# Strided scaling into token order, whole-tile stores, and a 384/128 split of the last rows, in a sliding-window attention + SwiGLU kernel

## The chip, the cores and the metric

The kernel runs on one core of a Trainium2 chip. The metric is device time in microseconds (us) of one execution; smaller is better. The five engines are named as in the profile: PE (matrix multiply), PEld (its weight loads), DVE (vector engine), ACT (scalar engine), POOL (GpSimd), SP (the engine that only issues transfers here). A "q" after a name (SPq, ACTq) is that engine's instruction queue.

## What is computed

```python
# q, k, v: (8 batches, 8 heads, 576 positions, 64), fp32
scores = q @ k.T / sqrt(64), kept where 0 <= i - j < 64, else -1e9
attn   = softmax(scores) @ v                      # (8, 8, 576, 64)
x      = attn with heads joined                   # (4608 tokens, 512)
g      = x @ w_gate ; val = x @ w_val             # (4608, 1536)
out    = (g * sigmoid(g) * val) @ w_out           # (4608, 512), fp32
```

## The kernel before

The 4608 tokens are nine tiles of 512. Tile 0 to 6 take the first 512 positions of batches 0 to 6, tile 7 (`LAST`) takes the last 64 positions of all eight batches, and tile 8 takes the first 512 positions of batch 7. Each tile passes through three stages:

1. **Attention.** `scores` (line 244) makes the exponentials of the scores, `sums` (309) or `sums_wide` (318) the reciprocal row sums `r`, and `mix_all` (371) multiplies the exponentials by the values. Its result `ao_ps` lies in PSUM as fp32, one 128x512 piece for each of four pairs of heads `u` (two 64-wide heads on the 128 partitions, 512 tokens along the columns). `scale` (356) then multiplies each piece by `r`, on DVE, into the bf16 tile `xT[t][:, u, :]`. One line does it, 359.
2. **Gate and value.** `gate_value` (397) runs for `m` = 0 to 11: four matmuls of 512 columns with `wg` and four with `wv` (line 401), one for each `c` = `u` of `xT`; ACT applies silu (394), and DVE multiplies into `hT` (395). The first four matmuls of a tile therefore need the four scaled pieces in the order in which they are made.
3. **Projection.** `project` (434) runs for four groups `s` of 128 of the tile's columns: twelve 512-column matmuls with `hT` as weights (410), a copy out of PSUM into `os_` (417), and stores to DRAM (429).

The order is written out by hand (`manual_schedule`). For t = 2 to 8 the loop (lines 652 on) interleaves tile t's attention with tile t-1's projection: `scores(t, 0)`, `project(t-1, 0)`, part of `s = 1`, `scores(t, 1)`, `sums`, the rest of `s = 1`, `project(t-1, 2)`, `sums`, `mix_all(t)`, `project(t-1, 3)`, and then the twelve `gate_value(t, m)`. So the four scales of a tile run on DVE while PE runs the twelve matmuls of `project(t-1, 3)`. For t = 1 the interleaving is written out (lines 638 to 650): behind `mix_all(1)` there are eight projection matmuls (`columns(10, 12)`), then four copies of tile 0's results, two on ACT and two on DVE, and then the gates. Tile 0 is the start of the pipeline, before the loop.

**Order of tokens.** The columns of a tile are not in token order. Tile 0 keeps e-major order with 4 tokens to a group (column = e * 128 + r for token 4r + e). All later tiles (`t >= TURNED`) use 16 (column = e * 32 + r for token 16r + e), which comes from the way the queries are loaded and turned. That order goes on through `ao_ps`, `r`, `xT`, `hT` and the result. A group of 128 columns thus holds four sets of 32 tokens whose rows in DRAM lie 16 apart, and `project_end` (415) writes each group with four stores of 32 rows. All are issued by SP, except that tile 8 alternates SP and ACT.

**The end.** The last 128 columns of tile 8 go through `project_last` (439): two halves of 256 output columns, twelve matmuls each (446), a copy each (450), and four stores of 32 rows each, alternating SP and ACT (453).

PSUM has two buffers each for the tags `g` and `v` (gates, projection) and two double ones for `a` (scores, mixing). `os_` and `r` have four buffers each.

Two operations elsewhere matter for reading the profile: `split_k` (188) copies bf16 from PSUM on DVE with a step of 128 elements in its source, and `turn_k` (207) and `turn_q` (194) transpose 32x32 blocks on DVE, the first with a step of 4 elements in its destination, the second contiguous there. Lines 496 and 612 read the small bf16 tile `tri` in SBUF with a step of 4 and of 16 elements.

Of the kernel before, what the change touches and what calls it, by code (L numbers as in the profile page):

```python
# [8 lines left out]
P = 128  # L9
# [8 lines left out]
def kernel(  # L18
# [10 lines left out]
    nc = tc.nc  # L29
    S, D, H = 576, 64, 8  # L30
    NTOK, DFF, DM = 4608, 1536, 512
    NT = NTOK // 512
    TURNED = 1
    LAST = NT - 2

    ctx.enter_context(tc.manual_schedule())
    cst = ctx.enter_context(tc.tile_pool(name="cst", bufs=1))
# [11 lines left out]
    wo = cst.tile([P, 12, DM], BF16, name="wo")  # L49
# [12 lines left out]
    def batch(t):  # L62
        return t if t < LAST else t - 1

# [6 lines left out]
    staged, queries, weights, inverse, xT, hT = {}, {}, {}, {}, {}, {}  # L71
# [9 lines left out]
    def load_q(t):  # L81
# [3 lines left out]
        for a, c in quarters:  # L85
            p0 = 64 * a + 32 * c
            if t != LAST:
                nc.gpsimd.dma_start(  # L88
# [26 lines left out]
    def load_qk(t):  # L115
        q_s = load_q(t)
        if t == 1:
            staged[t] = q_s, None
            return
        if t == LAST:  # L120
            groups = [(b, S - P) for b in range(4)]
# [122 lines left out]
    def scores(t, w):  # L244
# [3 lines left out]
        for j in range(8):  # L248
            if t == LAST:
                k_j = kT[t % 2 if j < 4 else 2]  # L250
# [4 lines left out]
            for lo, hi, c, src, k0 in pieces:  # L255
                for h in range(2):
                    for x in range(2):
# [11 lines left out]
                        )  # L269
        n = 1024 if t == LAST else 960  # L270
        for h in range(2):
# [8 lines left out]
            both = epool.tile([P, 8, 64], BF16, name="both", tag="both")  # L280
            lo = 2 if t == LAST else 0
            nc.vector.tensor_add(both[:], E[:, 1:17:2], E[:, lo:lo + 15:2])  # L282
# [17 lines left out]
    def room(n):  # L300
        return fsb.tile([P, 2, 512], FP32, name="r", tag="r", bufs=4)[:, 0:n]
# [54 lines left out]
    def scale(t, u, o_ps):  # L356
        if u == 0:
            xT[t] = att.tile([P, 4, 512], BF16, name="xT", tag="xT")
        nc.vector.tensor_mul(xT[t][:, u, :], o_ps, inverse.pop((t, u)))  # L359

    def values_first(u, o_ps):
        mix_first(u, o_ps)
        scale(0, u, o_ps)

    def wide(name):
        return ps_a.tile([P, 2, 512], FP32, name=name, tag="a")
# [4 lines left out]
    def mix_all(t):  # L371
        tiles = wide("ao_ps"), wide("ao_ps")
        for w in range(2):
            mix(t, w, (tiles[w][:, 0], tiles[w][:, 1]))
        for u in range(4):
            scale(t, u, tiles[u // 2][:, u % 2])
# [38 lines left out]
    def project_end(t, s, o_ps, copy=nc.vector.tensor_copy):  # L415
        os_ = fsb.tile([P, 512], FP32, name="os_", tag="os_", bufs=4)
        copy(os_[:], o_ps[:])
        rows = out[S * batch(t):S * batch(t) + 512]
        if t < TURNED:
            nc.sync.dma_start(rows.rearrange("(r e) f -> e r f", e=4)[s], os_[:])  # L420
            return
        if t == LAST:
            rows = out.rearrange("(b s) f -> b s f", s=S)[:, 512:S]
            rows = rows.rearrange("b (r e) f -> e b r f", e=16)
        else:
            rows = rows.rearrange("(r e) f -> e r f", e=16)
        for i in range(4):
            eng = nc.scalar if t == NT - 1 and i % 2 else nc.sync
            eng.dma_start(rows[4 * s + i], os_[32 * i:32 * i + 32])

    def out_tile():
        return ps_f.tile([P, 512], FP32, name="o_ps", tag="g")

    def project(t, s):
        o_ps = out_tile()
        project_part(t, (s,), (o_ps,), range(12))
        project_end(t, s, o_ps)

    def project_last(t, s):
        rows = out[S * batch(t):S * batch(t) + 512].rearrange("(r e) f -> e r f", e=16)  # L440
        os_ = fsb.tile([P, 512], FP32, name="os_", tag="os_", bufs=4)
        tiles = out_tile(), out_tile()
        for x in range(2):
            f = slice(256 * x, 256 * x + 256)
            for c in range(12):
                nc.tensor.matmul(  # L446
                    tiles[x][:, 0:256], hT[t][:, c, P * s:P * s + P], wo[:, c, f],
                    start=(c == 0), stop=(c == 11),
                )
            nc.vector.tensor_copy(os_[:, f], tiles[x][:, 0:256])  # L450
            for i in range(4):
                eng = nc.scalar if i % 2 else nc.sync
                eng.dma_start(rows[4 * s + i][:, f], os_[32 * i:32 * i + 32, f])

    def set_exp():
        nc.scalar.preload_act_table_set("natural_log_exp_and_others")  # L456
# [27 lines left out]
    for a in range(2):  # L484
        tr = tri[64 * a:64 * a + 64]
        nc.gpsimd.affine_select(
            out=tr[:, 1 - a], in_=tr[:, 1 - a], compare_op=ALU.is_ge, fill=0.0,
# [3 lines left out]
            out=tr[:, a], in_=tr[:, a], compare_op=ALU.is_ge, fill=0.0,  # L491
# [78 lines left out]
    d_ps, r = wide("d_ps"), room(2)  # L570
# [33 lines left out]
    for m in range(12):  # L604
# [15 lines left out]
        if 5 <= m < 9:  # L620
            u = m - 5
            join(on_a, keys[:, u], raw_k[:, 2 * u:2 * u + 2])
        if 6 <= m < 10:
            u = m - 6
# [8 lines left out]
    tiles = [ps_f.tile([P, 512], FP32, name="o_ps", tag=x) for x in "gvgv"]  # L633
# [15 lines left out]
    for s in range(4):  # L649
        project_end(0, s, tiles[s], on_a if s < 2 else on_v)  # L650

    for t in range(1, NT):
        if t > 1:
            set_exp()
            scores(t, 0)
            project(t - 1, 0)
            if t == 2:
                stage_v(3)
            o_ps = out_tile()
            project_part(t - 1, (1,), (o_ps,), range(5))  # L660
            scores(t, 1)
            sums(t, 0)
            project_part(t - 1, (1,), (o_ps,), range(5, 12))
            project_end(t - 1, 1, o_ps)
            project(t - 1, 2)
            sums(t, 1)
            mix_all(t)
            project(t - 1, 3)
# [21 lines left out]
    for s in range(3):  # L690
        project(NT - 1, s)
    project_last(NT - 1, 3)

# [28 lines left out]
```

## Time and profile before

| | us |
|---|---|
| median of three runs | 328.64 (328.26 to 329.04) |
| profiled execution, its own time: span from first to last instruction | 326.2 |
| median less span (what lies around the span) | 2.4 |
| PE busy | 315.9 (97%), 2700 matmuls |
| DVE busy | 220.2 (67%) |
| ACT busy | 167.2 (51%) |
| POOL busy | 142.8 (44%) |

The three timed runs list only their times; the profiled execution has no listed time beside its span, so the 2.4 us is taken as constant. The granted TensorE clock is 0.999 of full speed over the span. The chain of work that ended last runs 86% through PE; DMA has 8%, POOL 3% and DVE 1%. PE's busy time counts pipelined matmuls whose ends are modelled, so gaps are best read from starts: in the gates and projections one 512-column matmul follows another every 0.216 us (four take 0.86 us in the chain).

### The profile page before, as it was taken

To read this page: it belongs to the slowest core of one execution; us is meant where nothing else is said; L and a number is where in the kernel's file an instruction comes from. 1 tells how busy PE (TensorE), PEld (TensorE's weight loads), DVE (VectorE), ACT (ScalarE), POOL (GpSimd) and SP (SyncE) were. 2 spreads that over 40 slices of the span, in tenths; PEclk is the share of its full clock that TensorE was granted. 3 is DMA by queue.
4 is the path that set the end of the run, shared out by engine and by line. 5 is a ranking of instruction groups with operands and counts; after the bars stand their busy time and mean duration, and the time that the engine had idled before them with its cause. 6 is when DMAs were issued, how large, how long until landed. Compare 5 with 4: busy or idle time off the path is not lost.

```text
span 326.2 us, 6959 instructions
## 1 busy us (share of the span) xinstructions
PE 315.9 (97%) x2700; PEld 150.7 (46%) x2743; DVE 220.2 (67%) x352; ACT 167.2 (51%) x239; POOL 142.8 (44%) x256
## 2 busy tenths in 40 slices
PE   8899999999999999999999999999999999999995
PEld 3444444444444444444444544454444544444443
DVE  5865755587766776887678766876697586773431
ACT  5855557337733683358336743565347633773300
POOL 5944545986085893586024989464200000000000
PEclk9999999999999999999999999999999999999999
DMA  7999999999789999959812999799401300020013
GB/s 253 200 202 202 206 146 215 170 146 143 164 160 206 138 151 205 192 81 214 175 38 29 169 173 92 53 191 195 97 2 34 99 0 2 16 83 32 2 33 98
DMA packets 82865, 40.84 MB, mean 125 GB/s; under 512 B 64272, under 2 KB 78352, under 8 KB 82832
## 3 DMA queue, kind: packets, MB, share of 16 engines
q0 software_dynamic: 50672, 23.08, 57.7%
q1 hardware_dynamic: 31136, 16.26, 19.3%
q10 hardware_dynamic: 1024, 1.05, 1.1%
q8 instruction: 21, 0.34, 0.4%
q14 instruction: 12, 0.10, 0.1%
HBM read 54.00 MB, written 9.44 MB: 194 GB/s over the span
## 4 chain that ended last, share of the span: by engine, by line
PE 86%; DMA 8%; POOL 3%; issue 1%; DVE 1%; SPq 0%; DVEq 0%; POOLq 0%
PE o_ps L410 28%; PE g_ps L401 26%; PE v_ps L401 25%; DMA wv<-in_moe_w_val_dram 4%; DMA q_s<-in_q_dram 3%; PE s_ps L261 3%; PE ao_ps L347 2%; PE d_ps L294 1%; DMA q_f<-in_q_dram 1%; POOL wg L172 1%; POOL wv L172 1%; PE o_ps L446 1%; POOL v L129 1%; POOL qk_b L517 0%; DVE qT L198 0%
## 5 line engine op out<-in xcount | busy, mean ns | idle before, releaser
L394 ACT ACTIVATE sg<-g_ps 128x512 f32<-128x512 f32 x108 | 64.4, 597 | 113.8 <-PE g_ps L401 85.1
L395 DVE TENSOR_TENSOR hT<-sg,v_ps 128x512 bf16<-128x512 f32 x108 | 74.7, 693 | 59.8 <-PE v_ps L401 49.2
L401 PE MATMUL g_ps<-xT,wg 128*128 128x512 bf16 x415 | 108.2, 379 | 0.9
L401 PE MATMUL v_ps<-xT,wv 128*128 128x512 bf16 x415 | 107.2, 379 | 0.1
L410 PE MATMUL o_ps<-wo,hT 128*128 128x512 bf16 x396 | 93.6, 380 | 1.5 <-issue 0.3
L108 POOL DMA_DIRECT2D k_s<-in_k_dram x112 | 60.6, 552 | 26.2 <-DMA q_s<-in_q_dram 15.3
L401 PEld LDWEIGHTS <-wv 128*128 128x128 bf16 x424 | 41.5, 98 | 50.1
L401 PEld LDWEIGHTS <-wg 128*128 128x128 bf16 x424 | 41.3, 98 | 49.5 <-issue 0.6
L410 PEld LDWEIGHTS <-hT 128*128 128x128 bf16 x420 | 39.1, 98 | 46.5 <-issue 1.8
L274 ACT ACTIVATE eb<-s_ps 128x960 bf16<-128x960 f32 (+1 forms) x32 | 29.5, 974 | 16.4 <-PE s_ps L261 16.3
L208 DVE STREAM_TRANSPOSE kT<-k_s 128x512 bf16<-128x512 bf16 x28 | 36.0, 1284 | 0.3 <-issue 0.3
L277 DVE TENSOR_TENSOR eb<-eb,mask 128x960 bf16<-128x960 bf16 (+1 forms) x32 | 21.1, 658 | 14.4 <-ACT eb L274 14.4
L359 DVE TENSOR_TENSOR xT<-ao_ps,r 128x512 bf16<-128x512 f32 x36 | 23.0, 684 | 6.5 <-PE ao_ps L347 4.8
L162 POOL CAST vb<-v_f 128x512 bf16<-128x512 f32 x20 | 11.4, 618 | 31.9 <-DMA v_f<-in_v_dram 22.1
L304 ACT ACTIVATE r<-d_ps 128x512 f32<-128x512 f32 (+1 forms) x33 | 20.8, 629 | 6.2 <-PE d_ps L294 5.9
L198 DVE STREAM_TRANSPOSE qT<-q_s 128x512 bf16<-128x512 bf16 x32 | 22.4, 702 | 0.8 <-DMA q_s<-in_q_dram 0.8
L307 ACT ACTIVATE r<-r 128x512 f32<-128x512 f32 (+1 forms) x33 | 22.0, 669 | 1.0
L88 POOL DMA_DIRECT2D q_s<-in_q_dram x28 | 15.2, 564 | 10.2 <-DVE qT L198 4.8
L137 POOL DMA_DIRECT2D vb<-in_v_dram x16 | 10.9, 710 | 8.7 <-DMA wo<-in_moe_w_out_dram 3.7
L282 DVE TENSOR_TENSOR both<-eb 128x512 bf16<-128x512 bf16 x32 | 13.6, 425 | 1.1
L456 ACT ACT_TABLE_LOAD x9 | 11.5, 1283 | 2.0 <-issue 1.9
L95 POOL DMA_DIRECT2D q_s<-in_q_dram x16 | 8.6, 629 | 7.4 <-DVE qT L198 7.4
(107 smaller groups left out, 185.2 us busy)
## 6 DMA issues: line engine op xcount, KB each, us to landing
q_s<-in_q_dram POOLq DMA_DIRECT2D x28, 248.0 KB, 6.0
k_s<-in_k_dram POOLq DMA_DIRECT2D x112, 56.0 KB, 4.8
v_f<-in_v_dram SPq DMA_DIRECT2D x40, 128.0 KB
wo<-in_moe_w_out_dram POOLq DMA_DIRECT2D x3, 512.0 KB, 12.3
q_f<-in_q_dram SPq DMA_DIRECT2D x4, 256.0 KB
vb<-in_v_dram POOLq DMA_DIRECT2D x16, 64.0 KB, 2.9
v<-in_v_dram POOLq DMA_DIRECT2D x16, 64.0 KB, 3.1
q_s<-in_q_dram POOLq DMA_DIRECT2D x16, 62.0 KB, 3.6
```

The lines of the kernel that those rows point to most:

```text
L108: nc.gpsimd.dma_start(k_s[p0:p0 + 32, g, :, 0:w], k[b, a:H:2, s:s + P].rearrange("u (r e) d -> r u (e d)", e=4) [:, :, 32 * c:32 * c + w],)
L198: nc.vector.transpose(queries[t][:, u, :].rearrange("r (e x) -> r e x", e=16), staged[t][0][:, u].rearrange("r (e d) -> r e d", d=D)[:, :, ...
L208: nc.vector.transpose(dst[:, u, :].rearrange("r (g x e) -> r g e x", g=4, e=4), k_s[:, :, u].rearrange("r g (e d) -> r g e d", d=D)[:, :, ...
L274: nc.scalar.activation(flat, s_ps[h][:].rearrange("r a b -> r (a b)")[:, 0:n], AF.Exp, scale=0.125)
L277: nc.vector.tensor_mul(flat, flat, mask[:].rearrange("r j c e y -> r (j c e y)")[:, 0:n])
L304: nc.scalar.activation(r, d_ps, AF.Ln)
L307: nc.scalar.activation(r, r, AF.Exp, scale=-1.0)
L359: nc.vector.tensor_mul(xT[t][:, u, :], o_ps, inverse.pop((t, u)))
L394: nc.scalar.activation(sg[:], g_ps[:], AF.Silu)
L395: nc.vector.tensor_mul(hT[t][:, m, :], sg[:], v_ps[:])
L401: nc.tensor.matmul(ps[:], w[:, c, P * m:P * m + P], xT[t][:, c, :], start=(c == 0), stop=(c == 3),)
L410: nc.tensor.matmul(o_ps[:], hT[t][:, c, P * s:P * s + P], wo[:, c, :], start=(c == 0), stop=(c == 11),)
```

## The change

There are three parts. (1) For t >= 1 `scale` reads both of its sources with a step of 32 fp32 elements (128 bytes) and writes `xT` in token order, contiguous. (2) Since the columns then are tokens in order, each group of 128 columns is 128 consecutive rows of the output (in tile 7, two runs of 64), and one store takes them (two in tile 7, and two halves in the cases of `HALVED`), all from SP. (3) The last group's output columns are taken as 384 and 128 instead of 256 and 256, with one store each from SP.

```diff
+    HALVED = [(1, 0), (1, 1), (1, 2), (1, 3), (2, 0)]
...
     def scale(t, u, o_ps):
         if u == 0:
             xT[t] = att.tile([P, 4, 512], BF16, name="xT", tag="xT")
-        nc.vector.tensor_mul(xT[t][:, u, :], o_ps, inverse.pop((t, u)))
+        x, r = xT[t][:, u, :], inverse.pop((t, u))
+        if t < TURNED:
+            nc.vector.tensor_mul(x, o_ps, r)
+            return
+        nc.vector.tensor_mul(
+            x.rearrange("r (x e) -> r x e", e=16),
+            o_ps.rearrange("r (e x) -> r x e", e=16),
+            r.rearrange("r (e x) -> r x e", e=16),
+        )
...
         if t < TURNED:
             nc.sync.dma_start(rows.rearrange("(r e) f -> e r f", e=4)[s], os_[:])
-            return
-        if t == LAST:
-            rows = out.rearrange("(b s) f -> b s f", s=S)[:, 512:S]
-            rows = rows.rearrange("b (r e) f -> e b r f", e=16)
+        elif t == LAST:
+            for i in range(2):
+                r0 = S * (2 * s + i) + 512
+                nc.sync.dma_start(out[r0:r0 + 64], os_[64 * i:64 * i + 64])
         else:
-            rows = rows.rearrange("(r e) f -> e r f", e=16)
-        for i in range(4):
-            eng = nc.scalar if t == NT - 1 and i % 2 else nc.sync
-            eng.dma_start(rows[4 * s + i], os_[32 * i:32 * i + 32])
+            n = 2 if (t, s) in HALVED else 1
+            for i in range(n):
+                r = slice(P // n * i, P // n * (i + 1))
+                nc.sync.dma_start(rows[P * s:P * s + P][r], os_[r])
...
     def project_last(t, s):
-        rows = out[S * batch(t):S * batch(t) + 512].rearrange("(r e) f -> e r f", e=16)
+        r0 = S * batch(t) + P * s
         os_ = fsb.tile([P, 512], FP32, name="os_", tag="os_", bufs=4)
-        tiles = out_tile(), out_tile()
-        for x in range(2):
-            f = slice(256 * x, 256 * x + 256)
+        for f0, f1 in ((0, 384), (384, 512)):
+            o_ps = out_tile()
             for c in range(12):
                 nc.tensor.matmul(
-                    tiles[x][:, 0:256], hT[t][:, c, P * s:P * s + P], wo[:, c, f],
+                    o_ps[:, 0:f1 - f0], hT[t][:, c, P * s:P * s + P], wo[:, c, f0:f1],
                     start=(c == 0), stop=(c == 11),
                 )
-            nc.vector.tensor_copy(os_[:, f], tiles[x][:, 0:256])
-            for i in range(4):
-                eng = nc.scalar if i % 2 else nc.sync
-                eng.dma_start(rows[4 * s + i][:, f], os_[32 * i:32 * i + 32, f])
+            nc.vector.tensor_copy(os_[:, f0:f1], o_ps[:, 0:f1 - f0])
+            nc.sync.dma_start(out[r0:r0 + P, f0:f1], os_[:, f0:f1])
```

## The prediction

> **What bounds the kernel now.** I read the page first: its busy shares and the chain.
>
> ```profile
> PE 315.9 (97%) x2700; PEld 150.7 (46%) x2743; DVE 220.2 (67%) x352; ACT 167.2 (51%) x239; POOL 142.8 (44%) x256
> ...
> PE 86%; DMA 8%; POOL 3%; issue 1%; DVE 1%; SPq 0%; DVEq 0%; POOLq 0%
> ```
>
> PE sets the end; a change gains only where it shortens PE's work, its waits or the tail, and loses wherever it makes PE wait. So I asked next for the waits of PE.
>
> ```profile
> PE s_ps L230 <- DVE kT L189: 1.1, 2, 1.0
> PE g_ps L381 <- DVE xT L359: 0.6, 1, 0.6
> PE o_ps L410 <- issue: 0.3, 2, 0.2
> ```
>
> The columns are total us, times, longest. From tile 1 on PE waits for no scale (the 0.6 is tile 0) and for no store. Merging stores has no PE wait to remove, and the scales are hidden. The timeline shows how well; first tile 2, then tile 1:
>
> ```profile
> 84.30 2.68 DVE L359 TENSOR_TENSOR xT<-ao_ps,r 128x512 bf16<-128x512 f32 x4 [0.16 <-PE ao_ps L347]
> 84.53 2.77 PE L410 MATMUL o_ps<-wo,hT 128*128 128x512 bf16 x11
> 85.62 0.63 ACT L307 ACTIVATE r<-r 128x512 f32<-128x512 f32 x1
> 87.13 1.03 PE L401 MATMUL g_ps<-xT,wg 128*128 128x512 bf16 x4
> 87.33 0.69 DVE L417 COPY os__1355<-o_ps 128x512 f32<-128x512 f32 x1 [0.35 <-PE o_ps L410]
> 89.12 0.69 DVE L395 TENSOR_TENSOR hT<-sg,v_ps 128x512 bf16<-128x512 f32 x1 [1.10 <-PE v_ps L401]
> ```
>
> ```profile
> 51.08 2.48 DVE L359 TENSOR_TENSOR xT<-ao_ps,r 128x512 bf16<-128x512 f32 x4 [3.82 <-PE ao_ps L347]
> 53.24 1.02 PE L401 MATMUL g_ps<-xT,wg 128*128 128x512 bf16 x4
> ```
>
> The columns are start, length, instruction. In tile 2 four scales run from 84.30 to 86.98 under the last projection. The gate starts at 87.13 and needs the fourth scaled piece only at its fourth matmul, three steps of 0.216 later, at 87.78. That leaves 0.80. The 2.68 includes a wait of the fourth scale for ACT's last reciprocal (85.62 + 0.63 = 86.25); back to back four take 2.48, as tile 1 shows, so a scale occupies (2.48 - 0.68) / 3 = 0.60. Tiles 3 to 6 and 8 repeat tile 2 to 0.01 us (tile 8: scales at 288.19, gate at 291.02); tile 7 has scales at 254.17 and gate at 257.12. Tile 1 has least: need at 53.24 + 0.65 = 53.89 against 51.08 + 2.48 = 53.56.
>
> **Part 1, the scale.** Let d be the added time of one scale. With 0.05 to release PE (the last matmul's end and the last copy's start lie that close in the tail), the fourth scale releases at S + 2.48 + 4d + 0.05, S being the first scale's start; PE wants it at G + 0.65, G being the gate's. The stall is 4d - 0.95 in tiles 2 to 6 and 8 (G - S = 2.83), 4d - 1.07 in tile 7 (2.95), 4d - 0.28 in tile 1 (2.16), never below zero. Up to d = 0.24 only tile 1 pays.
>
> No row shows an fp32 read in SBUF with a large step. The nearest, by length (L359 itself: 668/680/692):
>
> ```profile
> L208 DVE STREAM_TRANSPOSE kT<-k_s 128x512 bf16<-128x512 bf16 x28 | 36.0, 1284 | 0.3 <-issue 0.3
> L198 DVE STREAM_TRANSPOSE qT<-q_s 128x512 bf16<-128x512 bf16 x32 | 22.4, 702 | 0.8 <-DMA q_s<-in_q_dram 0.8
> L189 DVE COPY kT<-tp 128x512 bf16<-128x512 bf16 x8 | 5.5, 682 | 0.6 <-PE tp L186 0.6
> L450 DVE COPY os__4457<-o_ps 128x256 f32<-128x256 f32 x2 | 0.8, 424 | 1.5 <-PE o_ps L446 1.5
> ```
>
> ```profile
> 2.33 0.58 DVE L496 TENSOR_SCALAR bias<-tri 128x64 bf16<-128x64 bf16 x4 [0.47 <-POOL tri L486]
> 2.95 0.56 DVE L501 COPY bias<-bias 128x256 bf16<-128x256 bf16 x2
> ```
>
> ```profile
> 23.18 0.68 DVE L612 COPY mask<-tri 64x64 bf16<-64x64 bf16 x4
> 23.90 0.79 DVE L617 COPY mask<-mask 128x128 bf16<-128x128 bf16 x3
> ```
>
> - PSUM source: L189 reads PSUM with a step of 256 bytes and takes 682 ns for 512 elements, what contiguous 512-column fp32 copies take (L417, 691). So the strided `ao_ps` costs nothing, and d >= 0: a gain is excluded, because the scale already runs one element a step (512-column less 256-column copy is 267 ns for 256 elements, 1.04 each, 158 fixed; 158 + 533 = 691) and no reordering of fp32 improves on that.
> - Upper end: L208 against L198, the same transposition with a step of 8 bytes instead of none in its SBUF destination, costs 0.58 more for 512 elements. It is a write, but the only large price of a step in SBUF here.
> - SBUF source: L612 and L496 both read 64 bf16 elements of `tri`, L612 at a step of 32 bytes and L496 at 8. Start to start, L612 takes (23.90 - 23.18) / 4 = 0.180 and L496 (2.95 - 2.33) / 4 = 0.155: 25 ns more. Both are too short for one element a step (158 + 67 = 225 ns; the medians are 206 and 190), so they take two, and the 25 ns are spread over 32 steps: 0.78 each. Over 512 steps that is d = 0.40. Were it one a step, d = 0.20.
>
> I take d = 0.40: `r` lies in SBUF, its step of 128 bytes is larger than L612's, and the row with a large price lies above it. The range keeps 0 to 0.58.
>
> A rule speaks against this change. The Trainium skill, Vector Engine (DVE) Microarchitecture Reference, section "Measured stream behaviour on trn2", says that a DVE port to SBUF keeps full rate only while consecutive elements come in runs of two adjacent 4-byte words: 1.05 ns a column becomes 1.73 with one source hopping 4 KiB at every element, 2.50 with both stepping 24 words. By 1.73 d is an estimated 0.35 and the sum below 332.3 us; by 2.50 it is 0.74 and 344.7. No row of before shows it for fp32.
>
> Stalls at d = 0.40: 6 x 0.65 + 0.53 + 1.32 = 5.75 us. At 0.58: 6 x 1.37 + 1.25 + 2.04 = 11.5. At 0.20: 0.5.
>
> What queues behind: PE runs in order, so the waiting fourth matmul holds the whole gate stage. On DVE the copy L417 of the last projection moves back by 4d; it frees the PSUM buffer of the second gate, needed 1.73 after the first plus the stall, and at either d it ends 0.4 before that. DVE then lags PE by 4d less the stall, 0.95, and L395 has 1.10 idle ahead of it. In tile 1 two copies on DVE (0.60 apart) free the second gate's buffers 0.4 before use at d = 0.40. So no second stall.
>
> **Part 2, stores.** For t >= 1 there were 132 stores, and are 42. 90 issues of some 0.42 us, 38 us of queue time, nearly all SP's, go. No PE or DVE instruction waits for a store. SP's `v_f` loads move earlier by up to a few us; POOL's casts wait for them (22.1 us), a whole tile before PE needs the values. Cost and gain nothing, while POOL has that slack; without it a late store or load would show as a wait of L347 or L417.
>
> **Part 3, the tail.**
>
> ```profile
> 321.47 2.09 SPq L453 DMA_DIRECT2D out_dram<-os__4457  x4
> 321.48 2.16 ACTq L453 DMA_DIRECT2D out_dram<-os__4457  x4
> 322.33 0.42 DVE L450 COPY os__4457<-o_ps 128x256 f32<-128x256 f32 x1 [0.89 <-PE o_ps L446]
> ```
>
> The 256-column matmuls come every 0.109 (24 in 2.63), 512-column ones every 0.216, so 384 take 0.163, twelve 1.95. The 128-column transposes (L186) come every 0.057 (four in 0.39, the last 0.22), twelve 0.68; together 2.63 again, or 0.5 more if the weight loads of 98 ns don't overlap. The last copy is 158 + 133 = 0.29, not 0.42: -0.13. Behind it SP issued two stores (about 0.78 in sum); one whole-tile store issues in 0.36 (L420: 0.35 to 0.40, once 1.27): -0.4. Sum -0.5, between -0.6 and +0.9 (slow issue, loads not hidden).
>
> **Sum.** Span 326.2 + 5.75 - 0.5 = 331.45; the median stands 2.44 above the span, giving 333.9 us.
>
> **Rivals.**
> - *The strided read of `r` is free* (d below 0.24, decided at 4d = 0.95). For: L189; L612 and L496 differ in operation, and 25 ns is little. Against: L208. Then only the tail is left: 328.64 - 0.5 = 328.1, at d = 0.20 328.6. This is the side not slower; 35%.
> - *The read costs as L208's write*: 328.64 + 11.5 - 0.5 = 339.6, and 341.0 with the tail at its bad end. 20% at or above some 337.
> - *The change doesn't do what it says for the stores*: 128-row stores take SP 1.27 us each as once in L420, and `os_` is freed late. DVE would wait at L417. 42 x 1.27 = 53 us of SP over 270 is still less than before's 55, so nothing during the tiles, +0.9 in the tail; slower by about 0.7 at most; 3%.
>
> **How the numbers follow.** The forecast (d from 0.3 to 0.5) has 42%, and is the likeliest; its own range is 331 to 337. Differences under 0.2% (0.66 us) can't be told from none. Free reads split around that limit: 22% faster, 13% same; with 1% same from small prices, slower has 64%. The range leaves out a fifth: from 327.8 (the tail's 0.6 and 0.2 for the scatter of the runs) to 341.0.
>
> **What would show it.** L359 at about 1.08 us instead of 0.68 (rival: 0.68; 1.26); a new wait of L401 on xT of 0.5 to 0.7 in seven tiles and 1.3 in the first; L417 and L395 without new waits; last matmul to end of span 0.5 shorter. L359 unchanged, or PE waiting for xT less than 4d - 0.95 says, would make the prediction wrong.

## The result and the profile after

The changed kernel takes 332.01 us (median of 6 runs, 331.36 to 333.56) against 328.66 (6 runs) for the kernel before: ratio 1.0112, 95% interval 1.0090 to 1.0134. It is slower, as forecast, by 3.4 us instead of 5.3. The profiled span grew from 326.2 to 329.3. Each run's time lies 2.0 to 2.1 us above its own span; the 2.4 of the working ahead of the result sets a median against the span of what must be a faster execution, which does no harm, since only differences are used. Two of the six runs of the changed kernel lie 1.4 and 1.6 us above the median at the same granted clock, and the record doesn't show why.

The page of the changed kernel, its busy shares and the chain that ended last:

```profile
PE 317.6 (96%) x2700; PEld 150.7 (46%) x2743; DVE 230.0 (70%) x352; ACT 167.2 (51%) x239; POOL 142.8 (43%) x256
...
PE 74%; DMA 9%; DVE 7%; issue 4%; POOL 3%; SPq 1%; ACT 1%; DVEq 0%; POOLq 0%
```

DVE's busy time grew by 9.8 us, and DVE, 1% of the chain before, now holds 7% of it: the end runs through the scales. The scale's group and the wait of PE that did not exist before (total, times, longest):

```profile
L364 DVE TENSOR_TENSOR xT<-ao_ps,r 128x512 bf16<-128x512 f32 x32 | 31.0, 1032 | 5.1 <-PE ao_ps L348 4.8
```

```profile
PE g_ps L410 <- DVE xT L364: 2.7, 9, 0.6
```

One scale takes 1.032 us instead of 0.68. The 2.7 us understate what PE lost, since this view counts from the modelled end of the matmul before. Starts tell it better; the timeline of tile 2, then of tile 1 (start, length, instruction):

```profile
85.28 3.87 DVE L364 TENSOR_TENSOR xT<-ao_ps,r 128x512 bf16<-128x512 f32 x4 [0.16 <-PE ao_ps L348]
86.61 0.63 ACT L308 ACTIVATE r<-r 128x512 f32<-128x512 f32 x1
88.11 0.81 PE L410 MATMUL g_ps<-xT,wg 128*128 128x512 bf16 x3
89.07 0.68 DVE L426 COPY os__1349<-o_ps 128x512 f32<-128x512 f32 x1
89.21 0.38 PE L410 MATMUL g_ps<-xT,wg 128*128 128x512 bf16 x1 [0.28 <-DVE xT L364]
90.55 0.69 DVE L404 TENSOR_TENSOR hT<-sg,v_ps 128x512 bf16<-128x512 f32 x1 [0.80 <-PE v_ps L410]
```

```profile
50.98 3.83 DVE L364 TENSOR_TENSOR xT<-ao_ps,r 128x512 bf16<-128x512 f32 x4 [3.82 <-PE ao_ps L348]
53.14 0.59 PE L410 MATMUL g_ps<-xT,wg 128*128 128x512 bf16 x2
53.94 0.38 PE L410 MATMUL g_ps<-xT,wg 128*128 128x512 bf16 x1 [0.20 <-DVE xT L364]
54.86 0.38 PE L410 MATMUL g_ps<-xT,wg 128*128 128x512 bf16 x1 [0.55 <-DVE xT L364]
```

In tile 2 the gate's first three matmuls run, and the fourth, due at 88.11 + 0.65 = 88.76, starts at 89.21, after the fourth scale's end at 89.15: 0.45 lost. In tile 1 the third matmul already waits for its scale, and the fourth is due at 53.79 and starts at 54.86: 1.07 lost in all. The L404 line shows that DVE still idles 0.80 ahead of its next work for the gates (1.10 before), so nothing behind the scales became late.

The tail of the changed kernel:

```profile
323.61 2.78 PE L454 MATMUL o_ps<-wo,hT 128*128 128x384 bf16 x24
325.76 0.96 DVE L458 COPY os__4373<-o_ps 128x384 f32<-128x384 f32 x2 [1.26 <-PE o_ps L454]
326.34 0.81 SPq L459 DMA_DIRECT2D out_dram<-os__4373  x2
```

The last 24 matmuls take 2.78 as before. From their end (326.39) to the span's end are 2.96 us; before they were 3.93.

### The profile page after: what moved, and what is told of

Read it like the earlier page. It is cut to its first block, busy times and chain, and to the rows that moved or that the text cites. A ratio compares the mean times of both kernels' runs of the same rounds, so it can differ in the third digit from the quotient of the medians.

```text
span 329.3 us, 6839 instructions
## 1 busy us (share of the span) xinstructions
PE 317.6 (96%) x2700; PEld 150.7 (46%) x2743; DVE 230.0 (70%) x352; ACT 167.2 (51%) x239; POOL 142.8 (43%) x256
## 4 chain that ended last, share of the span: by engine, by line
PE 74%; DMA 9%; DVE 7%; issue 4%; POOL 3%; SPq 1%; ACT 1%; DVEq 0%; POOLq 0%
PE v_ps L410 24%; PE g_ps L410 24%; PE o_ps L419 19%; DVE xT L364 6%; DMA wv<-in_moe_w_val_dram 4%; DMA q_s<-in_q_dram 3%; PE s_ps L262 2%; DMA q_f<-in_q_dram 1%; PE d_ps L295 1%; POOL wg L173 1%; PE ao_ps L348 1%; DMA v_f<-in_v_dram 1%; SPq L138 1%; POOL wv L173 1%; PE o_ps L454 1%
## 5 line engine op out<-in xcount | busy, mean ns | idle before, releaser
L404 DVE TENSOR_TENSOR hT<-sg,v_ps 128x512 bf16<-128x512 f32 x108 | 74.8, 693 | 57.8 <-PE v_ps L410 49.1
L410 PE MATMUL g_ps<-xT,wg 128*128 128x512 bf16 x415 | 109.6, 379 | 3.7 <-DVE xT L364 2.7
L364 DVE TENSOR_TENSOR xT<-ao_ps,r 128x512 bf16<-128x512 f32 x32 | 31.0, 1032 | 5.1 <-PE ao_ps L348 4.8
```

Of the source, the lines that this page charges most:

```text
L364: nc.vector.tensor_mul(x.rearrange("r (x e) -> r x e", e=16), o_ps.rearrange("r (e x) -> r x e", e=16), r.rearrange("r (e x) -> r x e", e=16),
L404: nc.vector.tensor_mul(hT[t][:, m, :], sg[:], v_ps[:])
L410: nc.tensor.matmul(ps[:], w[:, c, P * m:P * m + P], xT[t][:, c, :], start=(c == 0), stop=(c == 3),)
```

## The experiments

Theory A was: the strided read in the scale is the whole loss (A1: of it, only the SBUF source), and the stores and the tail give back 1.0 us. The rivals put part of it into the stores, or into the strided PSUM source.

**1. The scale put back.**

```diff
-        nc.vector.tensor_mul(
-            x.rearrange("r (x e) -> r x e", e=16),
-            o_ps.rearrange("r (e x) -> r x e", e=16),
-            r.rearrange("r (e x) -> r x e", e=16),
-        )
+        nc.vector.tensor_mul(x, o_ps, r)
```

> The changed kernel with only the scale put back to contiguous reads (the rows of each 512-token tile then come out permuted; all work is still done). Theory A (the strided read in the scale is the whole loss, and stores and tail give the 1.0 us by which the tail shrank): scale 0.68 us, no wait of the gates on xT after tile 0, time 327.7 us, 0.3% under before. Rival B (the merged stores themselves cost, by moving transfers): scale 0.68 and time 328.7 or above.

Measured: ratio to before 0.9966 (0.9953 to 0.9978), 327.27 us, span 325.3.

```profile
L364 DVE TENSOR_TENSOR xT<-ao_ps,r 128x512 bf16<-128x512 f32 x32 | 20.4, 686 | 5.7 <-PE ao_ps L348 4.8 <-ACT r L305 0.4
```

PE has no wait for a scale behind tile 0. From tile 1 to tile 8 the copies and products ahead of the tail start 0.02 us from where they start in the kernel before, although SP's `v_f` loads start up to 3.7 us earlier, and the tail is 0.98 shorter. So the merged stores are worth nothing inside the tiles, neither way, and rival B falls.

**2. The scale alone.** The kernel before with only the strided `tensor_mul` of the change.

> The kernel before with only the strided scale (stores and tail as before, so rows come out permuted; all work is still done). Theory A: scale 1.03 us, gates wait 0.45 us in tiles 2 to 6 and 8, 0.33 in tile 7, 1.1 in tile 1: 4.15 us on 328.66, 332.8 us. Rival B: the scale's cost is partly hidden and the stores carry the rest: under 331.5.

Measured: ratio 1.0121 (1.0103 to 1.0139), 332.50 us, span 330.6.

```profile
L363 DVE TENSOR_TENSOR xT<-ao_ps,r 128x512 bf16<-128x512 f32 x32 | 31.1, 1036 | 5.1 <-PE ao_ps L347 4.8 <-ACT r L304 0.4
```

The scale alone adds 4.3 us to the span, and the stores and the tail of experiment 1 take 1.0 off: together some 3.4 against the 3.1 of the whole change. By medians, against 328.40 for the kernel before measured beside them, they are 4.1 and 1.1, together 3.0 against 3.35. The parts add up within 0.4 us, and the loss is the scale's.

**3. r in token order.** ACT makes the reciprocal row sums `r` in two steps, a logarithm (Ln) and an exponential. The Ln, which copies the row sums out of PSUM anyway, puts them in token order; only the PSUM source of the scale stays strided.

```diff
-            log(r, d[x])
+            log(r.rearrange("r (x e) -> r x e", e=16), d[x].rearrange("r (e x) -> r x e", e=16))
...
             o_ps.rearrange("r (e x) -> r x e", e=16),
-            r.rearrange("r (e x) -> r x e", e=16),
+            r.rearrange("r (x e) -> r x e", e=16),
```

(`sums_wide` likewise.)

> The changed kernel, but ACT's Ln reads the row sums from PSUM strided and writes r in token order, so that in the scale only the PSUM source is strided. Theory A1 (only the SBUF source pays; PSUM is free, as L189 suggested): scale 0.68, Ln at or near 0.59, time 327.7. Rival A2 (a strided fp32 source pays in PSUM too): scale 1.03, time 332. If ACT pays for the strided read, Ln grows; up to 0.35 us each stays hidden behind the slack of 0.8 us.

Measured: ratio 0.9963 (0.9950 to 0.9976), 327.34 us, span 325.6.

```profile
L367 DVE TENSOR_TENSOR xT<-ao_ps,r 128x512 bf16<-128x512 f32 x32 | 20.4, 686 | 5.7 <-PE ao_ps L351 4.8 <-ACT r L305 0.4
L305 ACT ACTIVATE r<-d_ps 128x512 f32<-128x512 f32 x30 | 17.7, 590 | 4.8 <-PE d_ps L295 4.7
```

Both the scale and the Ln read PSUM with a step of 128 bytes and take what they took contiguous, 0.686 (0.68 before) and 0.590 (0.590). This is the change without its cost, and it beats both kernels: 0.37% under before. The last scale of tile 2 ends 0.79 ahead of its matmul again: the scales run 2.68 from 84.70, to 87.38, and the gate starts at 87.52, so its fourth matmul is due at 88.17.

**4. Only r strided.** The PSUM source is read contiguous, r with the step of 32 words.

> The changed kernel, but the scale reads the PSUM source contiguous and only r strided (each token gets another token's reciprocal; the work is the same in amount). Theory A1 (SBUF alone pays): scale 1.03 us, as with both strided. Rival A2 (PSUM pays): 0.68. Rival A3 (each pays a part): between.

```profile
L364 DVE TENSOR_TENSOR xT<-ao_ps,r 128x512 bf16<-128x512 f32 x32 | 31.1, 1032 | 5.1 <-PE ao_ps L348 4.8 <-ACT r L305 0.4
```

1.032 us, the same as with both strided: A1 holds, and the two prices don't add because one of them is nothing. The one run took 331.92 us.

**5. The step in SBUF.** One profile gives eight steps, one for each tile: `e = 2 ** (9 - t)`, `r` read as "(e x) -> x e", everything else contiguous. It is one run, of 331.16 us.

> The changed kernel with the PSUM source read contiguous and r read with another step in each tile: 2, 4, 8, 16, 32, 64, 128, 256 words for t = 1 to 8 (values are paired wrongly; the work is the same in amount). Theory C1 (a read is dear when each access falls into another 16-byte stretch): 0.68 us at 2 words, 1.03 at all others. Rival C2 (any word that stands alone is dear): 1.03 at 2 words too. Rival C3 (small steps cost more than large ones): up to 1.4 at 8 to 32 words, falling towards 256; at 32 words it must be 1.03. The gate's stall should follow 4d - 0.95 in each tile (4d - 0.28 in tile 1, 4d - 1.07 in tile 7).

The scales of tiles 1 to 8, one line for each tile (least, median and greatest ns); the steps are 2, 4, 8, 16, 32, 64, 128 and 256 words:

```profile
L365 DVE TENSOR_TENSOR xT<-ao_ps,r x4: 681/681/692, 52.0 to 53.8; 128x512 bf16<-128x512 f32 x4
L365 DVE TENSOR_TENSOR xT<-ao_ps,r x4: 1067/1082/1108, 85.3 to 88.3; 128x512 bf16<-128x512 f32 x4
L365 DVE TENSOR_TENSOR xT<-ao_ps,r x4: 1066/1074/1078, 119.8 to 122.8; 128x512 bf16<-128x512 f32 x4
L365 DVE TENSOR_TENSOR xT<-ao_ps,r x4: 1004/1012/1026, 154.3 to 157.1; 128x512 bf16<-128x512 f32 x4
L365 DVE TENSOR_TENSOR xT<-ao_ps,r x4: 1025/1032/1040, 188.6 to 191.5; 128x512 bf16<-128x512 f32 x4
L365 DVE TENSOR_TENSOR xT<-ao_ps,r x4: 1019/1034/1056, 223.0 to 225.8; 128x512 bf16<-128x512 f32 x4
L365 DVE TENSOR_TENSOR xT<-ao_ps,r x4: 1024/1039/1056, 257.7 to 260.6; 128x512 bf16<-128x512 f32 x4
L365 DVE TENSOR_TENSOR xT<-ao_ps,r x4: 682/688/696, 292.1 to 294.1; 128x512 bf16<-128x512 f32 x4
```

A step of 8 bytes is free, one of 16 bytes is the dearest (0.40 over contiguous), one of 32 bytes costs 0.39, and from 64 to 512 bytes it is 0.33 to 0.36. C2 falls at the first line. C1 is right in kind but missed the last: at 256 words the read goes to and fro between only two places, each of which moves on by one word, and that is free again. C3 is right only within 0.07 us. These tiles also test the stall formula with other values of d. How much later a tile's first product starts than in the kernel before, less the same for the tile ahead of it, is 0.67 at d = 0.40 (formula 0.65), 0.62 at 0.39 (0.61), 0.38 at 0.33 (0.37), 0.47 at 0.35 in tiles 5 and 6 (0.45), 0.35 in tile 7 (0.35), and 0.00 in tile 8 (0). In tile 1, counted from its first scale to its products, it is 0.00 too (0).

**6. The step in PSUM.** The same steps in the PSUM source, r contiguous.

> The same with r read contiguous and the PSUM source read with steps of 2, 4, 8, 16, 32, 64, 128, 256 words for t = 1 to 8. Theory: no step in PSUM costs anything: 0.68 us in every tile, no wait of the gates. Rival: some steps (large ones, or small ones) pay as in SBUF and only 32 words happens to be free.

All 32 scales in one line, and PE waited for none of them (one run, 327.36 us):

```profile
L365 DVE TENSOR_TENSOR xT<-ao_ps,r x32: 681/682/693, 51.2 to 290.3; 128x512 bf16<-128x512 f32 x32
```

**7. Runs of words.** r in runs of 1 word in tile 1, and of 2, 4, 8, 2, 2, 2, 2 words in tiles 2 to 8, the starts of neighbouring runs 32, 32, 32, 64, 16, 8 and 4 words apart in tiles 2 to 8. All runs start on an even word of the row. It is one run, of 328.38 us.

> The changed kernel with the PSUM source contiguous and r read in runs of 1, 2, 4, 8 words 32 words apart in runs' starts for tiles 1 to 4 (starts 32 words apart), and in runs of 2 words with starts 64, 16, 8 and 4 words apart for tiles 5 to 8. Theory C1 or C2 (two neighbouring words share an access): 1.03 us in tile 1 and 0.68 in all others. Rival (the change of address itself costs, so the price falls with the length of the run): 1.03, 0.86, 0.77, 0.73 in tiles 1 to 4 and about 0.86 in tiles 5 to 8.

Tile 1, then tiles 2 to 8:

```profile
L365 DVE TENSOR_TENSOR xT<-ao_ps,r x4: 1028/1042/1058, 51.1 to 53.9; 128x512 bf16<-128x512 f32 x4
L365 DVE TENSOR_TENSOR xT<-ao_ps,r x28: 680/682/693, 85.4 to 291.3; 128x512 bf16<-128x512 f32 x28
```

Two neighbouring words are enough to read at full rate, with the next pair at any of the five distances tried; pairs that start on an odd word were not tried. The rival (a price for each change of address) is out. With tile 1 alone paying, its stall was 1.13, from its first scale to its last product; the formula gives 4 x 0.36 - 0.28 = 1.16.

**8. The tail.** Experiment 3's kernel with 256 and 256 output columns, one 128-row store each.

```diff
-        for f0, f1 in ((0, 384), (384, 512)):
+        for f0, f1 in ((0, 256), (256, 512)):
```

> The version with r in token order, but with the last output columns again as 256 and 256, one 128-row store each. Theory: of the 1.0 us by which the tail shrank, 0.13 is the shorter last copy and the rest the single store (one issue in place of two on each queue, fewer transfers to wait for): last copy 0.42 us, the time from the last matmul to the end 0.13 to 0.2 longer than with 384 and 128, time 327.5. Rival (the split is the gain): 328.0 or above.

```profile
319.45 2.78 PE L457 MATMUL o_ps<-wo,hT 128*128 128x256 bf16 x24
321.42 1.64 SPq L462 DMA_DIRECT2D out_dram<-os__4373  x2
322.27 0.42 DVE L461 COPY os__4373<-o_ps 128x256 f32<-128x256 f32 x1 [0.89 <-PE o_ps L457]
```

From the last matmul's end (322.23) to the span's end (325.3) are 3.1 us, 0.1 more than the 2.96 with 384 and 128 and 0.8 less than before. The time, 0.9965 (0.9952 to 0.9978) of before, 327.34 us, can't be told from experiment 3's. So of the tail's 1.0 us the single stores (one in place of four, all on SP) give some 0.85 and the split some 0.15.

## Why the prediction was right in sign and too high in size

**What bounds it, and where the change bites.** Right. PE sets the end; the four scales and the gate's fourth matmul are the place. With the measured d the prediction's formula gives the stalls it named: 4 x 0.35 - 0.95 = 0.45 in tile 2 (0.45 measured), 1.12 in tile 1 (1.07), and 6 x 0.45 + 0.33 + 1.12 = 4.15 in all (0.44 to 0.48 measured in tiles 2 to 6 and 8, 0.32 in tile 7). From the start of tile 1 to the end of tile 8 the changed kernel fell back by 4.2 us. Experiment 5 holds the formula at five values of d and also where it says zero.

**The price of the strided read** was the term that was mis-sized: d = 0.40 was taken, 0.35 was measured (1.032 less 0.68). Four scales in eight tiles multiply the error: 32 x 0.05 = 1.6 us of the 2.1 by which the span was forecast too long. The step of the working that failed is the last one of the pair L612 and L496: start-to-start times of 64-element operations, 25 ns apart and only four of each, were spread over 32 steps and carried on to 512, and from a step of 32 bytes to one of 128. The pair pointed to the right source and was 14% too high. Experiment 5 shows which part was off: at a step of 32 bytes, that of L612, the fp32 read costs 0.39, what the pair gave, and at 128 bytes 0.35. The prediction took the larger step to be no cheaper. That the pair came so near at its own step may be luck, since its two lines read bf16, differ in operation and in partitions, and were taken to read two elements a step; no run repeated them. The upper row, L208, measured a write in another operation, and no step here came near its 0.58.

The rule that was weighed, of the Trainium skill's page Vector Engine (DVE) Microarchitecture Reference ("Measured stream behaviour on trn2"), would have given d = 0.35 and 332.3 us as an estimate by its 1.73 ns; the runs gave 0.35 and 332.0. With the tail as measured the same sum gives 331.8. Its 2.50 ns is for both sources, or the destination, stepping 24 words, and no run here has that; with one SBUF source the dearest step, 4 words, costs 0.40 / 512 = 0.78 ns over the usual 1.04, some 1.8. Experiment 7 shows its pairs of words as free as it says. Experiment 5 shows two cases free that its rule on pairs would charge: single words 2 apart, and single words from two places in turn. For the second the same section notes a one-source operation that ran so at full rate. The first is what the skill's page SBUF — State Buffer ("Specifications (TRN2)") says of lines of 16 bytes that need two hits.

**PSUM free:** right, and for steps of 8 to 1024 bytes in fp32, for DVE's scale (experiment 6) as for ACT's Ln (experiment 3, one step).

**Nothing in the tiles from the stores, and no second stall:** right (experiment 1; the idle time ahead of L404). The working had less room than there was: DVE fell behind PE by 0.30 (1.10 to 0.80 of idle time), not by 0.95. The longer scales first used up the 0.20 for which the fourth one had waited for ACT and the 0.35 for which DVE had idled ahead of L417, which leaves 0.40 of the 0.95.

**The tail:** sized at -0.5, measured -0.98, so also mis-sized, by the rest of the 2.1 us. The copy gave the 0.13 that was worked out (0.42 to 0.29). The last issue ended 0.43 after the last copy instead of 0.89: -0.46, where -0.4 was expected. The step left out is what follows: from the last issue's end to the span's end 2.2 us instead of 2.6, another -0.39. Experiment 8 has 2.28 there, so some 0.31 of it came with the single stores and some 0.08 with the smaller last one; what happens in that time no run shows. With -0.98 in all, the bound of -0.6 was too tight, without effect here.

**The rivals.** The free read (35%) is out, by experiments 1, 2 and 4. The price of L208's write is out by the changed kernel's own scale (1.03 us, not 1.26) and by experiment 5. The third, stores that take SP long, is out: 128-row stores took some 0.33 us each on SP from tile 3 on. Two of the 64-row ones took 1.29 and 1.58, and no copy waited for them.

## What to carry to other kernels

A strided fp32 source of the vector engine had a price here that depends on the memory, 0.33 to 0.40 us for 512 words at most steps in SBUF and nothing in PSUM: put the reordering where the data leave PSUM, by an instruction that runs anyway, and read SBUF contiguous or in pairs of words. Before slowing an instruction that is hidden, work out its slack at the consumer that ends the wait, in place and for each stage: here 0.24 us on each of four instructions were free, and 0.35 were not. Merged stores were worth something only where the kernel ends.

## What was not expected of the hardware

- In SBUF, fp32 words 16 bytes apart are dearer (1.08 us for 512) than words 128 bytes apart (1.03), and words 8 bytes apart are free (0.68).
- Reading SBUF in turn from two places 1 KB apart is free (0.69), from four places 512 bytes apart it is not (1.04). No run was made to find the cause.
- ACT reads fp32 from PSUM at a step of 128 bytes at no cost (Ln 0.590 both ways), which made the reordering there free.
